# Low parts of the first network's hidden values: a subtraction on POOL or DVE replaced by an accumulating DMA, with the second layer one step later

## The chip, the cores and the metric

The kernel runs on one core of one Trainium2 chip. The metric is device microseconds of that core for one execution. Three executions of the kernel before took 1061.05, 1056.88 and 1058.72 us; their median is 1058.72 us.

## What is computed

The input `x` has two sequences of 3008 tokens with 256 features. The reference takes the real part of a two-dimensional Fourier transform and sends every token through two small networks:

```python
X = np.fft.fft(x, axis=1); X = np.fft.fft(X, axis=2); x = X.real     # 6016 tokens of 256
gate = 1 / (1 + np.exp(-(x @ w_gate))); val = x @ w_val              # 256 -> 1536, twice
x = (gate * val) @ w_out                                             # first network, 1536 -> 256
h = x @ w_in                                                         # 256 -> 2048
out = (h * np.cos(h)) @ w_out2                                       # second network, 2048 -> 256
```

The inputs are float32. TensorE is fed with `float32r` operands, which keep fewer bits, so each product is made of three matmuls: an operand is cut into a high part (the value rounded to `float32r`) and a low part (the value less its high part), and high times high, low times high and high times low are added up in PSUM.

## The kernel before, in words

**Fourier transform.** Up to about 85 us the core transforms the tokens in three stages (`stage_b` and `stage_c` are the last two); the last two blocks of `stage_c` are woven into the first two steps of the first network. The result stands in six tiles `eo` of 2 x 1004 columns, each of which holds 502 even and 502 odd combinations, that is, 1004 tokens.

**First network.** `step1(s)` runs once for each of 72 pairs (six token tiles, twelve blocks of 128 hidden features), s = 12 t + f, and for a few steps more that drain it. Each step issues, on TensorE: `ab(s, 0)`, 6 matmuls of 502 columns (lines L474 to L476) for the even half; `ab(s, 1)`, 6 for the odd half; and `out1(s - L1)`, 12 matmuls (L516 and L517 on the high part of the hidden values, L514 on the low part) of the second layer for the block that was made L1 = 3 steps earlier. These are 24 matmuls a step.

Between the two layers the block s passes over the other engines:

- `even(s)` on DVE (L492, two instructions of 502 columns) takes the even half out of PSUM into `sas`.
- `tokens(s)` on DVE (L500, two instructions of 2 x 502 columns) adds and subtracts the odd half; the result `gv[s]` holds gate and value of 1004 tokens. It frees the PSUM banks that `ab(s + 1, 1)` writes. There are three `gv` buffers.
- ACT takes the sigmoid of the gate (L652, 1004 columns), in place.
- `times(s)` on POOL (L504, two of 502 columns) multiplies value and gate. It is issued in step s + 1.
- `hi1(s)` on ACT (L591, two of 502 columns) rounds the product into the high part `gh[s][:, 0]`, issued in step s + 1, right behind the two halves of `times(s)`.
- `lo1(s, c, at)` (L529, two of 502 columns) subtracts the high part from the product into the low part `gh[s][:, 1]`, in step s + 2, on POOL, or on DVE where the planner's clock of POOL is late (`e = V if ... else G`).

**The planner.** The order of instructions is made by the Python program itself. It keeps an estimated clock per engine (`clk`, advanced by `spend`), and between the fixed work of a step it calls `fill` (through `ahead`) to put steps of the weight preparation on an engine as long as they end by a given time. The weights come as eight-byte words and are turned into float32 on the chip: 34 units (twelve `w1`, six `wo1`, sixteen `w2`, and one small one), each with one load by SP's queue, two ACT instructions (L117, L118), three on DVE (L121, L123, L125), one on POOL (L128), and a split into high and low part on ACT (L133) and POOL or DVE (L134). A unit needs a room: one of `stages`, four pieces of the tile `D1`, three of which stay open for the whole first network; earlier units also use the `eo` tiles. `need` issues at once what is left of a unit when a step must have it: `wo1` unit u by the step L1 + 2 u. The `w2` units are written to DRAM (`ws`) and loaded over the first network's weights in the last twelve steps (`w2_load`).

**Second network.** 192 steps of 12 matmuls each (`hid`, L474 to L476 again, and `out2`, L558), with the cosine on ACT and DVE and the split on ACT and POOL.

The lines that the change touches are `gvs`, `sas`, `ks` and `rs` (pieces of `D1`), the rooms at the stage "b05", `tokens`, `lo1`, `hi1` and `step1`. The lines of `step1` around the change:

```python
if 1 <= s <= N1S:
    ahead(G, gate_at)
    for c in (0, PC):
        times(p, c)                       # p = s - 1
        done[c] = spend(G, 1.3, gate_at) + .1
    if s > 1:
        hi1(p)
```

Of the kernel before, what the change touches and what calls it, by code (L numbers as in the profile page):

```python
# [14 lines left out]
ALU = mybir.AluOpType  # L15
# [7 lines left out]
PC = 502  # L23
NCH = 3
NPT = B * NCH
TW = 2 * PC
# [5 lines left out]
NRAW = NPRE = 6  # L32
NWARM = 5
CX0 = 4
L1, L2 = 3, 5

INV2PI = float(np.float32(1 / (2 * np.pi)))
C1 = 6.28125
# [5 lines left out]
UC = 512  # L44
# [5 lines left out]
def fft_moe_moe(ctx: ExitStack, tc: tile.TileContext, x, x0, head, w1, w1s, wo1, w2, t1, t3, out):  # L50
# [10 lines left out]
    V, A, G, PE = nc.vector, nc.scalar, nc.gpsimd, nc.tensor  # L61

    def f32(ap):
        return ap.bitcast(F32)
# [21 lines left out]
    flat1 = D1.rearrange("p c j -> p (c j)")  # L86
    stages = [flat1[:, i * 3 * UC:(i + 1) * 3 * UC] for i in range(4)]

    GV0 = 9 * UC
    gvs = [flat1[:, GV0 + i * 2 * TW:GV0 + (i + 1) * 2 * TW] for i in range(3)]  # L90
    sas = flat1[:, GV0 + 6 * TW:GV0 + 7 * TW].rearrange("p (g c) -> p g c", g=2)
    ks = [gvs[0][:, i * PC:(i + 1) * PC] for i in range(2)]
    rs = [gvs[0][:, 2 * PC:3 * PC], gvs[0][:, 3 * PC:4 * PC], gvs[1][:, 0:PC]]

    ctx.enter_context(tc.manual_schedule())

# [5 lines left out]
    clk = {V: 0.0, A: 0.0, G: 0.0, DQ: 0.0}  # L102
    VG = (V, G)

    def spend(e, us, after=0.0):
        clk[e] = max(clk[e], after) + us
        return clk[e]
# [58 lines left out]
    live = []  # L166
    free = []
# [27 lines left out]
    def fill(e, until):  # L195

        while True:
            for un in live:
                step = un[2][0]
                if step[0] is VG and e is G and max(un[3], clk[V]) + VADV < max(un[3], clk[G]):  # L200
                    continue
                if e in step[0] if step[0] is VG else e is step[0]:
                    if max(un[3], clk[e]) + cost(step, e) <= until:
                        step_of(un, e)
                        break
            else:
                if e is DQ and len(todo) > held[0] and clk[e] + 1.5 <= until:
                    for bf in free:
                        if bf[2] <= until and max(clk[e], bf[2]) + LIFE <= bf[1]:
                            start(bf)  # L210
                            break
                    else:
                        return
                    continue
                return
# [6 lines left out]
    def finish(un):  # L222
        while un in live:
            step_of(un)

    def need(key):

        at = 0.0
        while key in todo:
            if not free:  # L230
                finish(live[0])
            start(free[0])
        for un in list(live):
            if un[0] == key:
                finish(un)
                at = un[3]
        return at

    LIFE, ALWAYS = 16.0, 1e9
    VADV = 0.5  # L240
    ENDS = (44, 52, 54, 62, 70, 70)

# [8 lines left out]
    def split_eo(t):  # L251
        live.insert(0, [("es", t), None, split_steps(ess[t % 2], eo[t][:, :, 0:PC]), 0.0])
# [24 lines left out]
    with tc.tile_pool(name="xp", bufs=1) as xp:  # L277
# [29 lines left out]
        now = 3.5  # L307
# [139 lines left out]
    for st in "b00 b01 b02 b03 b04 c00 b05 b10 c01 b11 c02 b12 b13 b14 c10 b15".split():  # L447
        kind, b, i = st[0], int(st[1]), int(st[2])
        if st == "c10":
            nbank[:] = [3, 4]  # L450
        now = (stage_b if kind == "b" else stage_c)(b, i)
        if st == "b01":
            after.append(consts)
        if st == "b05":
            free += [[bf, ALWAYS, now] for bf in stages[:3]] + [[stages[3], now + 24, now]]
            split_eo(0)


# [1 line left out]
    MM = .2275  # L460

    LATE = {V: 1.2, G: 4.5, A: 2.0}
    LO_BY = 5.0
    ES_AT, PSTART, PACE, NW2 = 3, 7, 16 / 58, 16
    ys = {}

# [12 lines left out]
    N1S = NPT * NF1  # L479
    gv, gh = {}, {}  # L480

    def ab(s, k):

        t, f = divmod(s, NF1)
        e = ess[t % 2]
        for g in range(2):
            three(ps[:, 4 + 2 * k + g, 0:PC], W1[:, f, g, k, 0], W1[:, f, g, k, 1], e[:, 0, k], e[:, 1, k])
# [7 lines left out]

    def tokens(s):

        gv[s] = gvs[s % 3].rearrange("p (g c) -> p g c", g=2)
        for c, op in ((0, ALU.add), (PC, ALU.subtract)):
            V.tensor_tensor(out=gv[s][:, :, c:c + PC], in0=sas, in1=ps[:, 6:8, 0:PC], op=op)  # L500

    def times(p, c):
        m = slice(c, c + PC)
        G.tensor_tensor(out=gv[p][:, 1, m], in0=gv[p][:, 1, m], in1=gv[p][:, 0, m], op=ALU.mult)  # L504
# [17 lines left out]
            else:  # L522
                A.copy(dst, src)

    def lo1(p, c, at):

        e = V if max(clk[G], at) + 1.3 > now + LO_BY and clk[V] < now + 12 * MM else G
        m = slice(c, c + PC)
        e.tensor_tensor(out=gh[p][:, 1, m], in0=gv[p][:, 1, m], in1=f32(gh[p][:, 0, m]), op=ALU.subtract)  # L529
        lo_at[p] = spend(e, 1.2 if e is V else 1.3, at) + .1  # L530


    def w2_load(u):
# [53 lines left out]

    def hi1(p):
        gh[p] = wp.tile([128, 2, TW], F32R, tag="gh", name=f"gh{p}", bufs=3)
        for c in (0, PC):  # L590
            A.copy(gh[p][:, 0, c:c + PC], gv[p][:, 1, c:c + PC])  # L591
            hi_at[p, c] = spend(A, .61, done[c]) + .1

    hi_at, done = {}, {}

    def ahead(e, until):
        fill(e, until + LATE[e])

    even_at = tokens_at = 0.0
    lo_at = {}  # L600

    def step1(s, mid=None):

        nonlocal now, gate_at, even_at, tokens_at
        main = s < N1S
        while after:
            after.pop(0)()

        held[0] = max(NW2 - max(PACE * (s - PSTART), 0), 0)
        fill(DQ, now + 3)  # L610
        if main:
            now = max(now, even_at, need(("w1", s)))
            if s % NF1 == 0:
                now = max(now, need(("es", s // NF1)))
            ab(s, 0)
        else:
            need(("ys", 0))
            i = s - N1S
            hid(i)
            cos_a(i)  # L620
        p = s - 1
        if 1 <= s <= N1S:

            ahead(G, gate_at)
            for c in (0, PC):
                times(p, c)
                done[c] = spend(G, 1.3, gate_at) + .1
            if s > 1:
                hi1(p)
        if main:  # L630

            ahead(V, now + 3 * MM)
            even(s)
            spend(V, .73, now + 3 * MM + .1)
            even_at = spend(V, .73, now + 6 * MM + .1) + .1
            now = mid() if mid else now + 6 * MM
            now = max(now, tokens_at)
            ab(s, 1)
            now += 6 * MM
        if 2 <= s <= N1S + 1:  # L640
            for c in (0, PC):
                lo1(s - 2, c, max(now, hi_at.pop((s - 2, c))))
            gv.pop(s - 2)
        if main:
            ahead(V, now)
            for un in [un for un in live if un[1] and un[1][1] < ALWAYS]:
                finish(un)
            free[:] = [bf for bf in free if bf[1] == ALWAYS]
            tokens(s)
            tokens_at = spend(V, 2.4, now + .1) + .1  # L650
            ahead(A, tokens_at)
            A.activation(out=gv[s][:, 0], in_=gv[s][:, 0], func=AF.Sigmoid)  # L652
            gate_at = spend(A, 1.05, tokens_at) + .1
        else:
            for e in (A, V, G):
                ahead(e, now)
        if s >= L1:
            now = max(now, lo_at.pop(s - L1, 0)) + 12 * MM
        if s >= L1:
            need(("wo1", (s - L1) // 2))  # L660
            ends = (s - L1) % NF1 == NF1 - 1
            out1(s - L1, 0, False)
            if ends:
                out1(s - L1, 0, True)
            out1(s - L1, 1, False)
            if not ends:
                out1(s - L1, 0, True)
            out1(s - L1, 1, True)
            gh.pop(s - L1)
        if main and s % NF1 == ES_AT and s // NF1 + 1 < NPT:  # L670
            split_eo(s // NF1 + 1)
            if s < NF1:
                live.append(live.pop(0))
        if s == N1S - 10:
            ys[0] = ess[0]
            live.insert(0, [("ys", 0), None, split_steps(ess[0], eo[0][:, :, 0:PC]), 0.0])
        if not main:
            if i >= 1:
                cos_b(i - 1)
            if i >= 2:  # L680
                cos_c(i - 2)


        while loads and s - (N1S - NF1) >= (loads[0] if loads[0] < NF1 else L1 + 2 * (loads[0] - NF1) + 1):
            u = loads.pop(0)
            need(("w2", u))
            w2_load(u)


    gate_at = 0.0  # L690
    LIFE, VADV = 0.0, 100.0
    beside[0] = .5
    free[:] = [bf for bf in free if bf[1] == ALWAYS]
    step1(0)
    now = stage_c(1, 1, AHC)
# [3 lines left out]
    free[:] = [bf for bf in free if bf[1] == ALWAYS]  # L699
    wp = ctx.enter_context(tc.tile_pool(name="wp", bufs=1))  # L700
    ess.append(wp.tile([128, 2, 2, PC], F32R, name="es1"))
    hi1(0)
    for s in range(2, N1S + L1):
        step1(s)
    for s in range(L1, N2S + L2):
# [102 lines left out]
```

## Time and profile before

| quantity | value |
|---|---|
| median of three executions | 1058.72 us (1056.88 to 1061.05) |
| the profiled execution, its own time | 1058.09 us |
| its span, first to last instruction | 1056.2 us |
| TensorE busy | 1011.9 us, 96% |
| DVE, ACT, POOL busy | 850.2, 715.9, 754.6 us |
| mean granted TensorE clock | 0.983 of full speed |

The profile is of one execution. Spans count from its first instruction. A matmul's row is about 0.39 us long, but the matmuls overlap in the pipeline, so it is the distance of their starts that tells how fast they go. "PEclk" is the share of full clock that TensorE was granted. In a table by stages, "(x87)" counts the instructions that touch a stretch, and in a row of a timeline the square bracket tells how long the engine had been idle before and what it waited for.

### The profile page before, as it was taken

Reading aid. Unit: us, or ns where it says so; the run is one execution under the profiler, and the core shown is the slowest. Engines: PE = TensorE matmul, PEld = TensorE weight load, DVE = VectorE, ACT = ScalarE, POOL = GpSimd, SP = SyncE. Lnnn points to the kernel's source line nnn. Section 1 sums busy time; section 2 is a strip of 40 time slices with the busy share of each in tenths; the row PEclk is TensorE's granted clock in tenths of the full one; section 3 lists DMA queues with packets and bytes.
Section 4 is the critical chain, followed back from the end, with each engine's and each line's share of the span. In section 5 each row is a group of like instructions: output and inputs, shape, how many; then the busy total and the mean of one; then the engine's idle time right before and its main releaser. Section 6 shows DMA issues by size and latency. Waiting matters only on the chain.

```text
span 1056.2 us, 13156 instructions
## 1 busy us (share of the span) xinstructions
PE 1011.9 (96%) x4566; PEld 837.4 (79%) x4566; DVE 850.2 (80%) x1087; ACT 715.9 (68%) x1208; POOL 754.6 (71%) x538
## 2 busy tenths in 40 slices
PE   9888977998989999999999999999999999999998
PEld 9877856887777777878788888888888888888886
DVE  4699984899999999999977777777777777777775
ACT  4665442545445545464588988889888898888886
POOL 2687995898999898989946656557565565665753
PEclk9899997999999999999999999999999999999999
DMA  9621010012121112053400000000000000000000
GB/s 259 205 100 61 0 40 21 1 40 80 40 80 41 40 40 81 1 159 119 159 22 3 17 20 1 21 20 1 20 1 20 20 0 20 1 20 20 1 20 21
DMA packets 15587, 48.57 MB, mean 46 GB/s; under 512 B 2016, under 2 KB 5408, under 8 KB 15520
## 3 DMA queue, kind: packets, MB, share of 16 engines
q1 hardware_dynamic: 15296, 47.59, 13.8%
q8 instruction: 36, 0.59, 0.2%
q14 instruction: 31, 0.25, 0.1%
q10 hardware_dynamic: 224, 0.14, 0.0%
HBM read 33.16 MB, written 14.56 MB: 45 GB/s over the span
## 4 chain that ended last, share of the span: by engine, by line
PE 66%; DVE 14%; POOL 8%; issue 7%; ACT 3%; DMA 2%; DVEq 0%; SPq 0%; POOLq 0%; ACTq 0%
PE ps L558 25%; PE ps L474 11%; PE ps L475 10%; PE ps L476 10%; DVE D L500 6%; POOL D L504 5%; DVE D L492 3%; POOL gh L529 3%; PE ps L514 3%; PE ps L516 2%; PE ps L517 2%; DMA eo<-in_w_dram 2%; DVE gh L529 1%; ACT D L652 1%; PE ps L417 1%
## 5 line engine op out<-in xcount | busy, mean ns | idle before, releaser
L584 POOL TENSOR_TENSOR h<-D,h 128x502 fp32r<-128x502 f32 x191 | 288.5, 1510 | 209.5 <-ACT h L583 205.0
L558 PE MATMUL ps<-h,wr 128*128 128x502 f32 x1152 | 291.8, 389 | 0.0
L474 PE MATMUL ps<-es,wr 128*128 128x502 f32 x672 | 265.2, 395 | 13.8 <-DVE D L500 13.6
L475 PE MATMUL ps<-es,wr 128*128 128x502 f32 x672 | 262.5, 391 | 0.0
L476 PE MATMUL ps<-es,wr 128*128 128x502 f32 x672 | 261.3, 389 | 0.0
L558 PEld LDWEIGHTS ps<-h,wr 128*128 128x128 f32 x1152 | 217.4, 189 | 44.7
L504 POOL TENSOR_TENSOR D<-D 128x502 f32<-128x502 f32 x144 | 204.0, 1437 | 41.9 <-ACT D L652 41.9
L591 ACT CAST gh<-D 128x502 fp32r<-128x502 f32 x144 | 88.1, 614 | 199.1 <-POOL D L504 184.5
L569 DVE SCALAR_TENSOR_TENSOR D<-D,ps 128x502 f32<-128x502 int32 x192 | 130.2, 678 | 113.0 <-POOL h L584 109.6
L500 DVE TENSOR_TENSOR D<-D,ps 128x1004 f32<-128x1004 f32 x144 | 172.2, 1196 | 11.9 <-PE ps L476 6.4
L474 PEld LDWEIGHTS ps<-es,wr 128*128 128x128 f32 x672 | 127.0, 189 | 48.4 <-DVE D L500 22.0
L570 DVE SCALAR_TENSOR_TENSOR D<-D 128x502 f32<-128x502 int32 x192 | 145.6, 759 | 6.6
L476 PEld LDWEIGHTS ps<-es,wr 128*128 128x128 f32 x672 | 126.8, 189 | 26.6
L475 PEld LDWEIGHTS ps<-es,wr 128*128 128x128 f32 x672 | 127.1, 189 | 24.9
L568 ACT ACTIVATE D<-ps 128x502 int32<-128x502 f32 x192 | 113.0, 589 | 41.5 <-PE ps L476 39.5
L576 DVE TENSOR_TENSOR D<-D,ps 128x502 f32<-128x502 f32 x192 | 128.9, 672 | 12.8 <-ACT D L575 12.8
L574 ACT ACTIVATE D<-D 128x502 f32<-128x502 f32 x192 | 119.3, 621 | 15.3 <-DVE D L570 12.7
L516 PE MATMUL ps<-gh,wr 128*128 128x502 f32 x288 | 115.2, 400 | 13.8 <-ACT wr L133 10.7
L575 ACT ACTIVATE D<-D 128x502 f32<-128x502 f32 x192 | 120.2, 626 | 6.1
L529 POOL TENSOR_TENSOR gh<-D,gh 128x502 fp32r<-128x502 f32 x92 | 123.9, 1360 | 0.0
L492 DVE SCALAR_TENSOR_TENSOR D<-eo,w,ps 128x502 f32<-128x502 f32 x144 | 100.1, 732 | 23.7 <-PE ps L476 21.8
L583 ACT CAST h<-D 128x502 fp32r<-128x502 f32 x192 | 114.9, 598 | 0.2 <-DVE D L576 0.2
(87 smaller groups left out, 1123.3 us busy)
## 6 DMA issues: line engine op xcount, KB each, us to landing
D<-in_w_dram SPq DMA_DIRECT2D x17, 512.0 KB, 3.3
ws<-D SPq DMA_DIRECT2D x16, 512.0 KB, 2.6
wr<-ws SPq DMA_DIRECT2D x16, 512.0 KB, 3.7
out_dram<-D SPq DMA_DIRECT2D x24, 251.0 KB, 2.9
raw<-in_x_dram SPq DMA_DIRECT2D x15, 384.0 KB, 9.4
eo<-in_w_dram SPq DMA_DIRECT2D x11, 512.0 KB, 9.1
D<-in_wo_dram SPq DMA_DIRECT2D x6, 512.0 KB, 5.0
T<-in_t_dram SPq DMA_DIRECT2D x1, 320.0 KB, 10.6
```

The source lines that it names most:

```text
L474: PE.matmul(o, w_hi, m_hi, start=first, stop=False)
L475: PE.matmul(o, w_lo, m_hi, start=False, stop=False)
L476: PE.matmul(o, w_hi, m_lo, start=False, stop=last)
L492: V.scalar_tensor_tensor(out=sas[:, g], in0=eo[t][:, 0, PC:TW], scalar=w128[:, g * NF1 + f:g * NF1 + f + 1], in1=ps[:, 4 + g, 0:PC], op0=A ...
L500: V.tensor_tensor(out=gv[s][:, :, c:c + PC], in0=sas, in1=ps[:, 6:8, 0:PC], op=op)
L504: G.tensor_tensor(out=gv[p][:, 1, m], in0=gv[p][:, 1, m], in1=gv[p][:, 0, m], op=ALU.mult)
L516: PE.matmul(o, WO1[:, f, 0, m], h[:, 0, sl], start=(f == 0), stop=False)
L529: e.tensor_tensor(out=gh[p][:, 1, m], in0=gv[p][:, 1, m], in1=f32(gh[p][:, 0, m]), op=ALU.subtract)
L558: PE.matmul(o, WO2[:, f, i, d * 128:(d + 1) * 128], h[:, m], start=(f == 0 and i == m == 0), stop=(f == NF2 - 1 and m == 1))
L569: V.scalar_tensor_tensor(out=r, in0=k, scalar=-C1, in1=h, op0=ALU.mult, op1=ALU.add)
L570: V.scalar_tensor_tensor(out=r, in0=k, scalar=-C2, in1=r, op0=ALU.mult, op1=ALU.add)
L584: (V if s == N2S - 1 else G).tensor_tensor(out=h[:, 1], in0=r, in1=f32(h[:, 0]), op=ALU.subtract)
```

## The change

`lo1` no longer subtracts. ACT writes the high part and, in a second instruction, the negated product rounded in the same way, which is the negated high part, into the place of the low part; then an accumulating DMA, issued by POOL, adds the product itself onto it, which leaves the product less its high part. Each of the three is made once per step with 1004 columns (502 KB for the DMA). `hi1` and `lo1` of a block are issued two steps after the block's `ab` (`hi1` was issued one step after it). The second layer runs 4 steps behind the first rather than 3. The `gv` buffers are four and begin at the third of the four rooms of `D1`, so that two rooms stay open for weights; the other two are open up to step 1, and what stands in them is finished in step 2. The pieces that the second network's cosine uses move along.

```diff
--- before.py
+++ after.py
@@ -32,7 +32,7 @@
 NRAW = NPRE = 6
 NWARM = 5
 CX0 = 4
-L1, L2 = 3, 5
+L1, L2 = 4, 5
 
 INV2PI = float(np.float32(1 / (2 * np.pi)))
 C1 = 6.28125
@@ -86,11 +86,12 @@
     flat1 = D1.rearrange("p c j -> p (c j)")
     stages = [flat1[:, i * 3 * UC:(i + 1) * 3 * UC] for i in range(4)]
 
-    GV0 = 9 * UC
-    gvs = [flat1[:, GV0 + i * 2 * TW:GV0 + (i + 1) * 2 * TW] for i in range(3)]
-    sas = flat1[:, GV0 + 6 * TW:GV0 + 7 * TW].rearrange("p (g c) -> p g c", g=2)
-    ks = [gvs[0][:, i * PC:(i + 1) * PC] for i in range(2)]
-    rs = [gvs[0][:, 2 * PC:3 * PC], gvs[0][:, 3 * PC:4 * PC], gvs[1][:, 0:PC]]
+
+    GV0 = 6 * UC
+    gvs = [flat1[:, GV0 + i * 2 * TW:GV0 + (i + 1) * 2 * TW] for i in range(4)]
+    sas = flat1[:, GV0 + 8 * TW:GV0 + 9 * TW].rearrange("p (g c) -> p g c", g=2)
+    ks = [gvs[2][:, i * PC:(i + 1) * PC] for i in range(2)]
+    rs = [gvs[2][:, 2 * PC:3 * PC], gvs[2][:, 3 * PC:4 * PC], gvs[3][:, 0:PC]]
 
     ctx.enter_context(tc.manual_schedule())
 
@@ -237,6 +238,7 @@
         return at
 
     LIFE, ALWAYS = 16.0, 1e9
+    TWO = 1e8
     VADV = 0.5
     ENDS = (44, 52, 54, 62, 70, 70)
 
@@ -452,7 +454,7 @@
         if st == "b01":
             after.append(consts)
         if st == "b05":
-            free += [[bf, ALWAYS, now] for bf in stages[:3]] + [[stages[3], now + 24, now]]
+            free += [[bf, ALWAYS, now] for bf in stages[:2]] + [[bf, TWO, now] for bf in stages[2:]]
             split_eo(0)
 
 
@@ -460,7 +462,6 @@
     MM = .2275
 
     LATE = {V: 1.2, G: 4.5, A: 2.0}
-    LO_BY = 5.0
     ES_AT, PSTART, PACE, NW2 = 3, 7, 16 / 58, 16
     ys = {}
 
@@ -495,7 +496,7 @@
 
     def tokens(s):
 
-        gv[s] = gvs[s % 3].rearrange("p (g c) -> p g c", g=2)
+        gv[s] = gvs[(s + 2) % 4].rearrange("p (g c) -> p g c", g=2)
         for c, op in ((0, ALU.add), (PC, ALU.subtract)):
             V.tensor_tensor(out=gv[s][:, :, c:c + PC], in0=sas, in1=ps[:, 6:8, 0:PC], op=op)
 
@@ -522,12 +523,10 @@
             else:
                 A.copy(dst, src)
 
-    def lo1(p, c, at):
-
-        e = V if max(clk[G], at) + 1.3 > now + LO_BY and clk[V] < now + 12 * MM else G
-        m = slice(c, c + PC)
-        e.tensor_tensor(out=gh[p][:, 1, m], in0=gv[p][:, 1, m], in1=f32(gh[p][:, 0, m]), op=ALU.subtract)
-        lo_at[p] = spend(e, 1.2 if e is V else 1.3, at) + .1
+    def lo1(p, at):
+
+        G.dma_start(out=f32(gh[p][:, 1]), in_=gv[p][:, 1], accum_op=ALU.add)
+        lo_at[p] = spend(G, 1.2, at) + 4
 
 
     def w2_load(u):
@@ -587,11 +586,11 @@
 
     def hi1(p):
         gh[p] = wp.tile([128, 2, TW], F32R, tag="gh", name=f"gh{p}", bufs=3)
-        for c in (0, PC):
-            A.copy(gh[p][:, 0, c:c + PC], gv[p][:, 1, c:c + PC])
-            hi_at[p, c] = spend(A, .61, done[c]) + .1
-
-    hi_at, done = {}, {}
+        A.copy(gh[p][:, 0], gv[p][:, 1])
+        A.mul(gh[p][:, 1], gv[p][:, 1], -1.0)
+        return spend(A, 2.1, done.pop(p)) + .1
+
+    done = {}
 
     def ahead(e, until):
         fill(e, until + LATE[e])
@@ -618,15 +617,17 @@
             i = s - N1S
             hid(i)
             cos_a(i)
-        p = s - 1
+        if 3 <= s <= N1S + 1:
+            hi_at = hi1(s - 2)
         if 1 <= s <= N1S:
 
             ahead(G, gate_at)
             for c in (0, PC):
-                times(p, c)
-                done[c] = spend(G, 1.3, gate_at) + .1
-            if s > 1:
-                hi1(p)
+                times(s - 1, c)
+                done[s - 1] = spend(G, 1.3, gate_at) + .1
+        if 3 <= s <= N1S + 1:
+            lo1(s - 2, hi_at)
+            gv.pop(s - 2)
         if main:
 
             ahead(V, now + 3 * MM)
@@ -637,15 +638,11 @@
             now = max(now, tokens_at)
             ab(s, 1)
             now += 6 * MM
-        if 2 <= s <= N1S + 1:
-            for c in (0, PC):
-                lo1(s - 2, c, max(now, hi_at.pop((s - 2, c))))
-            gv.pop(s - 2)
         if main:
             ahead(V, now)
-            for un in [un for un in live if un[1] and un[1][1] < ALWAYS]:
+            for un in [un for un in live if un[1] and un[1][1] < (TWO if s < 2 else ALWAYS)]:
                 finish(un)
-            free[:] = [bf for bf in free if bf[1] == ALWAYS]
+            free[:] = [bf for bf in free if bf[1] == ALWAYS or bf[1] == TWO and s == 0]
             tokens(s)
             tokens_at = spend(V, 2.4, now + .1) + .1
             ahead(A, tokens_at)
@@ -699,7 +696,8 @@
     free[:] = [bf for bf in free if bf[1] == ALWAYS]
     wp = ctx.enter_context(tc.tile_pool(name="wp", bufs=1))
     ess.append(wp.tile([128, 2, 2, PC], F32R, name="es1"))
-    hi1(0)
+    lo1(0, hi1(0))
+    gv.pop(0)
     for s in range(2, N1S + L1):
         step1(s)
     for s in range(L1, N2S + L2):
```

## Rows read from the trace of the kernel before

**Rows 1.** The page's first part: busy us (share of the span) xinstructions.

```profile
PE 1011.9 (96%) x4566; PEld 837.4 (79%) x4566; DVE 850.2 (80%) x1087; ACT 715.9 (68%) x1208; POOL 754.6 (71%) x538
```

**Rows 2.** Table by stages: stretch and length; busy (instructions) PE, PEld, DVE, ACT, POOL; PEclk; DMA.

```profile
85.00:108.00 23.00, 20.10 (x87) 15.72 (x87) 20.55 (x25) 13.07 (x21) 16.89 (x14) 1.00 0.20 69
108.00:150.00 42.00, 40.96 (x180) 33.38 (x179) 39.84 (x43) 20.45 (x30) 39.09 (x29) 1.00 0.04 13
150.00:185.00 35.00, 23.98 (x79) 18.21 (x79) 17.16 (x19) 10.09 (x16) 21.08 (x17) 0.76 0.10 31
185.00:510.00 325.00, 312.04 (x1350) 252.19 (x1349) 307.69 (x315) 160.42 (x229) 297.05 (x217) 1.00 0.18 61
510.00:531.00 21.00, 18.59 (x75) 14.64 (x74) 18.32 (x16) 10.25 (x16) 18.27 (x13) 0.92 0.52 180
531.00:1052.00 521.00, 521.00 (x2296) 431.93 (x2294) 387.29 (x573) 451.76 (x799) 311.40 (x202) 1.00 0.03 12
```

**Rows 3.** Waits of TensorE, 84 to 531 us: total us, times, longest.

```profile
PE ps L474 <- DVE D L500: 13.6, 14, 1.6
PE ps L516 <- ACT wr L133: 10.7, 2, 5.6
PE ps L516 <- ACT eo L523: 3.1, 4, 1.3
PE ps L514 <- POOL gh L529: 2.4, 2, 1.7
```

**Rows 4.** Timeline of DVE ahead of one of those waits: start us, us, instruction.

```profile
238.87 1.38 DVE L492 SCALAR_TENSOR_TENSOR D<-eo,w,ps 128x502 f32<-128x502 f32 x2
240.17 3.40 DVE L529 TENSOR_TENSOR gh<-D,gh 128x502 fp32r<-128x502 f32 x2
243.49 2.42 DVE L500 TENSOR_TENSOR D<-D,ps 128x1004 f32<-128x1004 f32 x2
```

**Rows 5.** Timeline of TensorE: that wait, and one for `wo1` weights.

```profile
155.49 0.79 PE L516 MATMUL ps<-gh,wr 128*128 128x502 f32 x1 [5.05 <-ACT wr L133]
...
245.97 0.49 PE L474 MATMUL ps<-es,wr 128*128 128x502 f32 x1 [1.40 <-DVE D L500]
```

**Rows 6.** Groups by line, 185 to 510 us: count | busy us, mean ns | idle before.

```profile
L504 POOL TENSOR_TENSOR D<-D 128x502 f32<-128x502 f32 x112 | 158.4, 1435 | 26.4 <-ACT D L652 26.4
L500 DVE TENSOR_TENSOR D<-D,ps 128x1004 f32<-128x1004 f32 x113 | 135.1, 1196 | 8.1 <-PE ps L476 4.0 <-DVE D L125 0.2 <-ACT eo L523 0.2
L529 POOL TENSOR_TENSOR gh<-D,gh 128x502 fp32r<-128x502 f32 x67 | 90.8, 1367 | 0.0
...
L492 DVE SCALAR_TENSOR_TENSOR D<-eo,w,ps 128x502 f32<-128x502 f32 x112 | 77.8, 732 | 9.8 <-PE ps L476 8.2
L591 ACT CAST gh<-D 128x502 fp32r<-128x502 f32 x111 | 68.2, 614 | 152.3 <-POOL D L504 148.9 <-PE ps L514 3.3
L529 DVE TENSOR_TENSOR gh<-D,gh 128x502 fp32r<-128x502 f32 x43 | 62.7, 1471 | 0.0
...
L652 ACT ACTIVATE D<-D 128x1004 f32<-128x1004 f32 x56 | 58.3, 1040 | 14.9 <-DVE D L500 14.4
...
L128 POOL TENSOR_TENSOR D<-D 128x512 int32<-128x512 int32 x14 | 20.6, 1474 | 0.0
L125 DVE SCALAR_TENSOR_TENSOR D<-D 128x512 uint32<-128x512 uint32 x15 | 20.4, 1357 | 0.0
L134 POOL TENSOR_TENSOR D<-D 128x512 fp32r<-128x512 f32 x14 | 19.6, 1403 | 3.2 <-ACT D L133 2.6
L123 DVE TENSOR_SCALAR D<-D 128x512 uint32<-128x512 uint32 x16 | 15.0, 937 | 0.0
...
L121 DVE TENSOR_SCALAR D<-D 128x512 f32<-128x512 f32 x16 | 10.5, 659 | 0.0
```

**Rows 7.** The page's DMA issues: engine, count, KB each, us to landing.

```profile
ws<-D SPq DMA_DIRECT2D x16, 512.0 KB, 2.6
```

**Rows 8.** Timeline of SP's queue: one such issue.

```profile
395.30 0.33 SPq L161 DMA_DIRECT2D ws<-D  x1
```

## The prediction

> **What bounds the kernel now.** I read the page's busy line first: TensorE 96% of the span, DVE 80%, POOL 71% [rows 1]. TensorE is the bound on average, so the question is where its other time lies, and the table by stages answers it [rows 2]. In the second network (531 to 1052 us) 2296 matmuls stand in 521 us, 0.227 us each, and TensorE is busy throughout: nothing is to be had there. At that pace the stages before it lose: 85 to 108 us, 23 - 87 x 0.227 = 3.3 us; 108 to 150, 1.1; 150 to 185, 17.1; 185 to 510, 18.5; 510 to 531, 4.0. That is 44 us in all, and the most that this change can give back.
>
> The waits of TensorE name the causes [rows 3]. A wait's row starts at the modelled end of a 0.39 us matmul, so each costs some 0.16 us more than it shows, and a long one also costs clock: 150 to 185 us, with the two waits for ACT's L133, had a mean granted clock of 0.76 [rows 2].
>
> - 14 waits for `tokens` on DVE (L500). Two belong to the first steps, and in the timeline all twelve later ones have the same picture: one or two of the subtractions of `lo1` (L529) stand on DVE between `even` and `tokens`. One of them is shown: 3.40 us of L529, then 2.42 us of L500, then TensorE 1.40 us late [rows 4, 5].
> - Two waits of over 5 us for a `wo1` weight unit that was not yet decoded when its step came [rows 3, 5]. DVE and POOL had no room for it: from 185 to 510 us they are busy 307.7 and 297.1 of 325 us [rows 2]. That is a consequence of the same subtractions, which take 62.7 us of DVE and 90.8 us of POOL there [rows 6].
> - Four waits for `eo` (L523), issued on ACT behind a late sigmoid, and two at the end for the last low parts on POOL [rows 3].
>
> So the first network is a TensorE-bound loop that stumbles over DVE and POOL.
>
> **The change part by part.** I count per step; 185 to 510 us holds 112 / 2 = 56 steps [rows 6], 5.80 us each, against 24 x 0.227 = 5.45 us of matmuls.
>
> *DVE* loses L529. What stays is (135.1 + 77.8) / 56 = 3.80 us of `tokens` and `even`, and (20.4 + 15.0 + 10.5) / 56 = 0.82 us of weights [rows 6]: 4.62 of 5.45 us, where it now has 307.7 / 56 = 5.49.
>
> *ACT* exchanges two casts of 0.614 us for two instructions of 1004 columns, for which I take the sigmoid's 1.04 us: (160.4 - 68.2) / 56 + 2.08 = 3.73 us [rows 2, 6]. It stays covered. `hi1` moves a step back, so that ACT no longer waits for `times` (148.9 us of idle time ahead of L591 [rows 6]), and the sigmoid behind it in the queue comes earlier.
>
> *POOL* loses its share of L529 and gains one DMA issue per step. Without L529 it has (297.1 - 90.8) / 56 = 3.68 us. What the issue takes of POOL stands in no row, since POOL issues no DMA now. Bounds: 0.33 us, what SP's queue takes for a plain one [rows 8], and 2.73 us, the two instructions of 1.367 us that it replaces [rows 6]. I take 1.3, nearest to one of these two, since one instruction takes the place of two: POOL has 4.98 of 5.45 us. The issue waits on POOL for ACT's two instructions; queued behind it are weight work and the next `times`.
>
> [...] The rows show that the only float32 instructions of DVE from SBUF to SBUF with one input are L121 and L123, 16 each in the stage, (0.659 + 0.937) x 16 = 25.5 us [rows 6]; no row shows one beside a DMA issued by POOL. [...]
>
> *The transfer.* 502 KB each step, read from two places and written to one. A plain 512 KB store lands 2.6 us after its issue [rows 7]. Three streams (two reads, one write) against its two make one and a half times that, 3.9 us, my value; bounds are 2.6 and, for three passes of full length, 7.8. The room: call the start of step p + 2 zero. Sigmoid and `hi1` end at about 2.9, the two `times` of the next block at 3.8, the issue at 5.1, the landing at 9.0. TensorE wants the low part in step p + 4 at 2 x 5.45 + 2.73 + 1.8 = 15.4. Even 7.8 us leaves 2 us. The extra step of distance pays for the DMA; the waits that come with it, `tokens` for the buffer of four steps ago and L514 for the transfer, lie behind that room.
>
> *The weights.* Two rooms instead of three. A unit is due every 3.6 steps (16 in 58), so each may stay 7 steps, some 39 us; with 0.8 us of DVE and 0.5 us of POOL left free in each step the planner finds place sooner than now. The `wo1` units are due a step later, too. I expect both long waits to go, and cost the lost room at nothing; the cover is that free time, and without it a late unit costs what it costs now, some 8 us (half of 17.1).
>
> *The edges.* In the first steps there is no second layer, and DVE's 3.8 us against 2.7 us of matmuls set the pace. That stage keeps its 3.3 us, and a fourth step without `out1` adds 3.8 + 0.2 - 2.7 = 1.3, say 1.5 us. At the end the last DMAs must land behind ACT's work for the second network, while the last weights load: 2 us stay of 4 (0 to 6).
>
> **The sum.** Lost after the change: 3.3 + 1.5 at the start, 0 from 108 to 185 us, 4 of the 18.5 us from 185 to 510 (stray waits for `tokens` behind weight work and for `eo`), 2 at the end, 10.8 us. 44.0 - 10.8 = 33.2 us saved. The profiled execution took 1058.09 us, 0.6 below the median of three: 1058.1 - 33.2 = 1024.9, so 1025 us. Of the bounds, no loss at all but the start's gives 1019; some spread below that is in the pace itself.
>
> **Rivals.**
>
> *POOL becomes the bound (slower).* The place is POOL's queue in every step. With 2.73 us for an issue it has 3.68 + 2.73 = 6.41 us a step. The steps from 108 to 510 us take 402 / 67 = 6.00 us now (1609 matmuls, 24 each [rows 2]), so it decides from an issue of 2.3 us on: 67 x 0.41 = 27 us more, 1085 us. For it: POOL is 91% busy now and nothing shows the price. Against: it needs the whole of what is removed. 0.08. Near 2.2 us it gives back all that was won, and the time stays within 0.5%: 0.05.
>
> *The transfer is the bound.* If the accumulation kept the DMA engines for the full 7.8 us, each step would wait for its transfer: 67 x 1.8 = 121 us more, 1179 us. For it: three passes; against: the engines are 18% busy in this stage now [rows 2], and a transfer that merely lands late is covered. 0.05.
>
> *The waits are only moved.* DVE's place between `even` and `tokens` is filled by weight work in place of L529, or the two rooms delay the units so that the last ones are forced through in the end. If the 18.5 us of 185 to 510 us stay: 1025 + 14.5 + 4 for the end, about 1043 us. Against it: the weight work on DVE is the same as now, and the picture of the twelve waits. 0.14.
>
> *Held-up issues.* [...] 0.06. [...]
>
> **How the numbers follow.** My forecast (1015 to 1038) has 0.62, the held-up issues 0.06, the moved waits 0.14, no change 0.05, the two slower cases 0.13. Faster by over 0.5% (about what a measurement of this kernel can tell from no change) is 0.62 + 0.06 + 0.14 = 0.82. The range runs from 1015, a little below the bound without waits, to 1048, which takes in the moved waits.
>
> **What would show it.** Right: no L529 on DVE; the waits for L500 down from 14 to a few; no wait for L133; a granted clock of 1.00 from 108 to 510 us; steps of 5.5 us. DVE about 75 us less busy, ACT some 60 us more. The POOL price is right if its other instructions start some 1.3 us later around an issue. Wrong: POOL's instructions back to back with gaps of over 2 us for an issue, TensorE waiting at L514 for the DMA, or at L516 for a weight unit; a start later than 3 us against now would say that closing the two rooms in step 2 costs something.

## The result and the profile after

The changed kernel takes 1043.6 us (median of 4 runs, 1041.4 to 1046.3) against 1059.4 us before: ratio 0.985, interval 0.982 to 0.989. It is faster by 15.8 us; I had forecast 33.2 us. The time lies above my forecast of 1015 to 1038 us and inside the wider range to 1048, which was set to take in a rival. The profiled execution took 1041.4 us (span 1039.5).

The page's busy line, to be read beside [rows 1]:

```profile
PE 1005.1 (97%) x4566; PEld 838.0 (81%) x4566; DVE 780.4 (75%) x1033; ACT 765.0 (74%) x1207; POOL 668.0 (64%) x521
```

The load moved as planned: DVE 69.8 us less, POOL 86.6 less, ACT 49.1 more. Both engines that stood in TensorE's way have room now. The table by stages (columns as in [rows 2]) shows how little of that arrived:

```profile
85.00:108.00 23.00, 19.14 (x84) 14.66 (x82) 21.24 (x26) 12.82 (x18) 13.25 (x11) 1.00 0.24 68
108.00:150.00 42.00, 38.41 (x158) 31.73 (x159) 35.40 (x39) 25.25 (x30) 33.06 (x30) 0.92 0.53 112
150.00:185.00 35.00, 35.00 (x155) 29.05 (x154) 28.87 (x35) 24.14 (x29) 26.70 (x24) 1.00 0.60 134
185.00:510.00 325.00, 315.39 (x1355) 258.94 (x1354) 246.97 (x263) 200.90 (x232) 237.07 (x208) 0.98 0.69 161
510.00:531.00 21.00, 21.00 (x94) 17.32 (x93) 14.24 (x21) 17.08 (x30) 8.64 (x6) 1.00 0.21 43
```

The stages are fixed stretches of time. The length of a stretch less its matmuls at 0.227 us, as in the prediction, gives what TensorE loses in it:

| stage, us | before | forecast | after |
|---|---|---|---|
| 85 to 108 | 3.3 | 4.8 (with the fourth step) | 3.9 |
| 108 to 150 | 1.1 | 0 | 6.1 |
| 150 to 185 | 17.1 | 0 | -0.2 |
| 185 to 510 | 18.5 | 4 | 17.4 |
| 510 to 531 | 4.0 | 2 | -0.3 |
| sum | 44.0 | 10.8 | 26.9 |

So the gain is in the main what the two long waits for `wo1` weights (150 to 185 us) and the end of the network cost before, less 5.0 us more lost from 108 to 150. In the 325 us of the long stage TensorE issues 1355 matmuls instead of 1350: hardly any gain, with DVE 60.7 us less busy there. TensorE's waits from 84 to 531 us:

```profile
PE ps L475 <- DVE D L501: 10.9, 6, 4.2
PE ps L475 <- DVE D L493: 5.3, 4, 2.9
PE ps L515 <- DMA gh<-D: 0.9, 1, 0.9
```

Against [rows 3] the waits for L133, for `eo` and for POOL's `gh` are gone, and the waits for `tokens` (now L501) went from 14 to 6, but they are longer, and four waits for `even` (L493) are new. What makes DVE late with so much room? One of the four places, first DVE (timeline: start us, us, instruction):

```profile
257.70 0.88 DVE L122 TENSOR_SCALAR D<-D 128x512 f32<-128x512 f32 x1
258.61 5.37 DVE L124 TENSOR_SCALAR D<-D 128x512 uint32<-128x512 uint32 x1
263.90 1.37 DVE L493 SCALAR_TENSOR_TENSOR D<-eo,w,ps 128x502 f32<-128x502 f32 x2
```

POOL in the same stretch:

```profile
257.62 1.19 POOL L528 DMA_DIRECT2D gh<-D  x1
258.22 1.70 POOL L135 TENSOR_TENSOR es<-eo,es 128x502 fp32r<-128x502 f32 x1
259.47 1.69 POOL L135 TENSOR_TENSOR D<-D 128x512 fp32r<-128x512 f32 x1
260.73 2.87 POOL L505 TENSOR_TENSOR D<-D 128x502 f32<-128x502 f32 x2
263.17 1.27 POOL L528 DMA_DIRECT2D gh<-D  x1
```

and TensorE behind it:

```profile
264.68 0.50 PE L475 MATMUL ps<-es,wr 128*128 128x502 f32 x1 [1.34 <-DVE D L493]
...
267.96 0.79 PE L475 MATMUL ps<-es,wr 128*128 128x502 f32 x1 [1.66 <-DVE D L501]
268.55 0.62 PE L476 MATMUL ps<-es,wr 128*128 128x502 f32 x1
268.96 0.62 PE L477 MATMUL ps<-es,wr 128*128 128x502 f32 x1
```

A weight instruction that elsewhere takes 0.43 us takes 5.37, and it ends 0.38 us after the last of four POOL computations that stand end to end (260.73 + 2.87 = 263.60). `even` and `tokens` stand behind it on DVE, so TensorE waits twice, and after the second wait its matmuls start 0.41 us apart instead of 0.23: the granted clock is 0.50 from 268 to 273 us, and 1.00 again from 276 to 280. Four rows are like that: L122 at 105.77 (3.42 us), L124 at 195.86 (4.58), L124 at 258.61 and L122 at 324.87 (5.42). By the starts of TensorE's matmuls, 2.9, 6.2 and 6.3 us are lost behind the last three, 15.4 of the 17.4 us of the long stage, and the loss of 108 to 150 us follows the first.

The other terms, in the groups of 185 to 510 us, beside [rows 6]:

```profile
L505 POOL TENSOR_TENSOR D<-D 128x502 f32<-128x502 f32 x112 | 145.3, 1358 | 75.2 <-ACT D L649 75.2
L590 ACT ACTIVATE gh<-D 128x1004 fp32r<-128x1004 f32 x57 | 59.3, 1040 | 0.0
L589 ACT CAST gh<-D 128x1004 fp32r<-128x1004 f32 x57 | 58.1, 1019 | 1.0 <-PE ps L515 1.0
L528 POOL DMA_DIRECT2D gh<-D x57 | 54.1, 949 | 12.2 <-issue 6.7 <-ACT D L573 3.1 <-POOL D L505 1.4
L124 DVE TENSOR_SCALAR D<-D 128x512 uint32<-128x512 uint32 x13 | 15.8, 1217 | 0.4
L122 DVE TENSOR_SCALAR D<-D 128x512 f32<-128x512 f32 x13 | 11.6, 892 | 0.7 <-ACT D L118 0.7
L126 DVE SCALAR_TENSOR_TENSOR D<-D 128x512 uint32<-128x512 uint32 x13 | 9.3, 714 | 0.0
```

An issue takes 0.95 us of POOL (I took 1.3), ACT's two instructions 1.02 and 1.04 us (I took 1.04). The transfer, in the page's list (beside [rows 7]) and in the view of L528:

```profile
gh<-D POOLq DMA_DIRECT2D x72, 502.0 KB, 4.7
```

```profile
DMA to landing us min/median/max: 4.4/4.7/10.1
```

4.7 us against the 3.9 that I took. From the start of an issue to the first low matmul there are 11.8 us in the median and 7.2 at the least, and TensorE waited for the transfer at one step (0.9 us, the last wait above).

### The profile page after: what moved, and what is told of

It reads as the page before. It is cut to its first block, busy times and chain, and to the rows that moved or that the text cites. A ratio compares the mean times of both kernels' runs of the same rounds, so it can differ in the third digit from the quotient of the medians.

```text
span 1039.5 us, 13150 instructions
## 1 busy us (share of the span) xinstructions
PE 1005.1 (97%) x4566; PEld 838.0 (81%) x4566; DVE 780.4 (75%) x1033; ACT 765.0 (74%) x1207; POOL 668.0 (64%) x521
## 4 chain that ended last, share of the span: by engine, by line
PE 73%; DVE 4%; ACT 2%; DMA 1%; issue 1%; POOL 0%; DVEq 0%; ACTq 0%
PE ps L557 25%; PE ps L475 12%; PE ps L476 12%; PE ps L477 12%; PE ps L515 4%; PE ps L517 4%; PE ps L518 4%; DVE D L501 3%; DMA gh<-D 1%; ACT gh L589 1%; DVE D L124 1%; DVE D L122 1%; ACT gh L590 1%; DVE D L493 0%; ACT eo L524 0%
## 5 line engine op out<-in xcount | busy, mean ns | idle before, releaser
L583 POOL TENSOR_TENSOR h<-D,h 128x502 fp32r<-128x502 f32 x191 | 284.3, 1489 | 215.8 <-ACT h L582 204.1
L475 PE MATMUL ps<-es,wr 128*128 128x502 f32 x672 | 265.6, 395 | 16.1 <-DVE D L501 10.9
L505 POOL TENSOR_TENSOR D<-D 128x502 f32<-128x502 f32 x144 | 186.3, 1352 | 93.0 <-ACT D L649 93.0
L501 DVE TENSOR_TENSOR D<-D,ps 128x1004 f32<-128x1004 f32 x144 | 172.9, 1201 | 51.6 <-PE ps L477 30.0
L649 ACT ACTIVATE D<-D 128x1004 f32<-128x1004 f32 x72 | 75.1, 1044 | 149.8 <-DVE D L501 149.8
L493 DVE SCALAR_TENSOR_TENSOR D<-eo,w,ps 128x502 f32<-128x502 f32 x144 | 101.8, 736 | 32.7 <-PE ps L477 32.3
L517 PE MATMUL ps<-gh,wr 128*128 128x502 f32 x288 | 114.3, 397 | 0.0
L518 PE MATMUL ps<-gh,wr 128*128 128x502 f32 x288 | 113.4, 394 | 0.0
```

Source lines behind the costliest of these rows:

```text
L475: PE.matmul(o, w_hi, m_hi, start=first, stop=False)
L517: PE.matmul(o, WO1[:, f, 0, m], h[:, 0, sl], start=(f == 0), stop=False)
L518: PE.matmul(o, WO1[:, f, 1, m], h[:, 0, sl], start=False, stop=False)
L583: (V if s == N2S - 1 else G).tensor_tensor(out=h[:, 1], in0=r, in1=f32(h[:, 0]), op=ALU.subtract)
```

## The experiments

The first theory: while POOL issues the accumulating DMA, or because of the way its instructions then stand (in the rows above each starts before the one ahead of it ends), DVE's `tensor_scalar` (L122 and L124, the clamp and the shift of the weight preparation) is kept from starting. The first four kernels test it.

**The same DMA as a plain copy, issued by SP.** The low part is then the whole product.

```diff
-        G.dma_start(out=f32(gh[p][:, 1]), in_=gv[p][:, 1], accum_op=ALU.add)
+        nc.sync.dma_start(out=f32(gh[p][:, 1]), in_=gv[p][:, 1])
```

> The transfer of each step is a plain copy of the product, issued by SP's queue; POOL issues no DMA (the low part is then the whole product). Theory: the lost time comes from POOL's issue, behind which POOL's rows overlap and DVE's TENSOR_SCALAR (L122, L124) gets no turn; without an issue on POOL no such row is longer than 1.6 us, the waits for L493 and L501 after 108 us are nearly gone, and the time is 1041.4 - 22 = about 1019 us (1014 to 1026). Rival, the transfer's traffic slows DVE: the same bytes still move each step, rows of 3 to 5 us stay and the time is 1036 to 1046. Rival, the place of the weight work in DVE's queue: 1036 to 1046 too, with short rows.

Measured: 1021.0 us, ratio 0.964 (0.961 to 0.967). No `tensor_scalar` takes over 1.41 us, and TensorE's waits from 84 to 531 us are down to

```profile
PE ps L475 <- DVE D L501: 4.2, 3, 2.0
PE ps L475 <- DVE D L493: 0.2, 1, 0.2
```

all in the first steps. The rows stay in the same place of DVE's queue and are short now, so neither that place nor the bytes moved each step made them long. With POOL free of the issue the rest of the change gives 1021 us, against the 1025 that I had forecast.

**A plain copy issued by POOL.** Same line, `G.dma_start` without `accum_op`; the low part is the whole product here too.

> The transfer is issued by POOL as in the changed kernel, but copies without adding (the low part is then the whole product). Theory: as in the changed kernel, some TENSOR_SCALAR rows of 3 to 5.5 us, POOL's rows overlapping by some 0.3 us behind an issue, 1036 to 1046 us. If the adding is what matters: no such rows, about 1019 us.

Measured: 1037.4 us, ratio 0.980 (0.977 to 0.983). The issue takes 0.58 us instead of 0.87 (medians), and the long rows are there again. DVE and then POOL:

```profile
321.03 5.45 DVE L122 TENSOR_SCALAR D<-D 128x512 f32<-128x512 f32 x1 [0.42 <-ACT D L118]
```

```profile
319.96 0.58 POOL L528 DMA_DIRECT2D gh<-D  x1 [1.62 <-issue]
320.56 1.29 POOL L135 TENSOR_TENSOR es<-eo,es 128x502 fp32r<-128x502 f32 x1
321.79 1.30 POOL L135 TENSOR_TENSOR D<-D 128x512 fp32r<-128x512 f32 x1
323.05 2.50 POOL L505 TENSOR_TENSOR D<-D 128x502 f32<-128x502 f32 x2
325.50 0.58 POOL L528 DMA_DIRECT2D gh<-D  x1
```

POOL's rows do not run into one another here (320.56 + 1.29 = 321.85, the next starts at 321.79), so the overlap is not the cause. The accumulation itself costs some 6 us (1043.6 - 1037.4).

**The subtraction on POOL, no DMA at all.** One instruction of 1004 columns; ACT's negated copy is dropped, and the planner's prices stay, so that the order of the rest does too.

```diff
-        G.dma_start(out=f32(gh[p][:, 1]), in_=gv[p][:, 1], accum_op=ALU.add)
+        G.tensor_tensor(out=gh[p][:, 1], in0=gv[p][:, 1], in1=f32(gh[p][:, 0]), op=ALU.subtract)
...
-        A.mul(gh[p][:, 1], gv[p][:, 1], -1.0)
```

> The changed kernel without the DMA and without ACT's negated copy: POOL subtracts, one instruction of 1004 columns; one step more of distance, four gate-value buffers, two rooms and the order stay. Theory: no TENSOR_SCALAR row over 1.6 us, since POOL issues no DMA; but POOL has 4.23 - 0.94 + 2.2 = 5.5 us a step against 5.45 and becomes the bound here and there, 1025 to 1045 us. Rival, any long run of POOL instructions keeps DVE out: rows of 3 us and more stay and are more frequent, over 1045 us.

Measured: 1095.1 us, ratio 1.034 (1.030 to 1.038), slower than both kernels. L122 now waits up to 10.4 us with no DMA on POOL:

```profile
PE ps L475 <- DVE D L493: 37.3, 10, 9.2
```

```profile
308.41 10.42 DVE L122 TENSOR_SCALAR D<-D 128x512 f32<-128x512 f32 x1
318.87 0.43 DVE L124 TENSOR_SCALAR D<-D 128x512 uint32<-128x512 uint32 x1
```

POOL's last row ahead of its end:

```profile
316.20 2.35 POOL L528 TENSOR_TENSOR gh<-D,gh 128x1004 fp32r<-128x1004 f32 x1
```

POOL has run without a gap from 305.43 to 318.55 us, and L122 ends 0.28 us later. The theory of the issue falls: the long rows need no DMA on POOL, and the rival stated beforehand (any long run of POOL's instructions keeps DVE out) is what came. What remains is POOL's computation: L122 waited here until it paused.

**The weights' two operations in a form with one operand in PSUM.** Two spare columns of a PSUM bank hold the second constants; the values are the same, and the new form holds from the first step of the first network on. The clamp, in part (`...` stands for lines left out):

```diff
+    cmax = ps[:, 7, 510:511]
...
+        if one_port[0]:
+            V.scalar_tensor_tensor(out=t, in0=t, scalar=FMIN, in1=cmax.to_broadcast([128, n]),
+                                   op0=ALU.max, op1=ALU.min)
...
-            (V, .34, lambda: V.tensor_scalar(out=t, in0=t, scalar1=FMIN, scalar2=FMAX,
-                                             op0=ALU.max, op1=ALU.min)),
...
+            (V, .34, lambda: clamp(t, n)),
...
+    one_port[0] = True
     step1(0)
```

and L124's shift in the same way.

> The changed kernel, but from the first network's first step on the two TENSOR_SCALAR of a weight unit are SCALAR_TENSOR_TENSOR with the second constant read from a spare PSUM column; the order of all instructions stays. Theory: these rows take 0.6 to 0.8 us and none is over 1.6, POOL is untouched, the waits of TensorE for L493 and L501 after 108 us nearly go, 1018 to 1026 us. Rival, the place of the weight work in DVE's queue or the two rooms: the waits stay, 1036 to 1046 us.

Measured: 1025.6 us, ratio 0.969 (0.966 to 0.972). The waits of TensorE, and the long stage of the table:

```profile
PE ps L492 <- DVE D L518: 6.5, 4, 2.0
PE ps L532 <- DMA gh<-D: 2.2, 2, 1.3
PE ps L492 <- DVE D L510: 0.2, 1, 0.2
```

```profile
185.00:510.00 325.00, 321.07 (x1406) 264.52 (x1405) 247.76 (x274) 209.33 (x247) 238.44 (x210) 1.00 0.69 162
```

1406 matmuls in the stage instead of 1355. By stages it loses 2.1 + 1.8 - 0.2 + 5.8 - 0.3 = 9.2 us, where the forecast had 10.8; the single terms differ by up to 2.7 us and partly cancel. The order of all instructions is that of the changed kernel, so the place of the weight work in DVE's queue, the rival here, is not what cost it. This version beats both kernels. The direction that the prediction had weighed, DVE holding up POOL's issues, cost nothing that shows: with the old form and with the new an issue takes 0.87 us and its transfer lands in 4.7 and 4.9 us (medians).

**The same form with the subtraction on POOL.** This was to separate two causes of the 1095 us.

> The kernel with POOL's subtraction of 1004 columns (1095.1 us, ten waits of TensorE for L493 on DVE, 37.3 us in all), with nothing altered but the form of the two DVE operations of the weight units: the second constant is read from a PSUM column, so that they run as scalar_tensor_tensor. Theory (a two-operation tensor_scalar from SBUF to SBUF is kept waiting by a long run of POOL's instructions, and everything behind it on DVE with it): the rows of 6.5 to 10.4 us are gone, the two new rows stay near 0.7 us each, the waits for L493 are under 5 us in all, and the time falls by at least 40 us, to 1055 us or less. Rival (POOL, with 2 x 1.28 + 2.40 us a step and its weight work, is simply too full for a step of 5.46 us, and DVE is late only as a consequence): TensorE still waits, now for POOL's L528, and the time stays above 1085 us.

Measured: 1078.3 us, ratio 1.019 (1.015 to 1.022). Neither expectation holds: 17 us came back, not 40, and TensorE's waits for `even` still are 28.6 us in all, and none is for POOL's subtraction. The groups of weight instructions on DVE, 95 to 531 us, say why. First POOL's subtraction with the old form, then with the new one:

```profile
L122 DVE TENSOR_SCALAR D<-D 128x512 f32<-128x512 f32 x19 | 79.9, 4206 | 6.6 <-ACT D L118 6.6
L126 DVE SCALAR_TENSOR_TENSOR D<-D 128x512 uint32<-128x512 uint32 x19 | 23.6, 1244 | 0.0
L124 DVE TENSOR_SCALAR D<-D 128x512 uint32<-128x512 uint32 x19 | 21.7, 1143 | 0.6
```

```profile
L143 DVE SCALAR_TENSOR_TENSOR D<-D 128x512 uint32<-128x512 uint32 x19 | 85.0, 4474 | 0.0
L123 DVE SCALAR_TENSOR_TENSOR D<-D,ps 128x512 uint32<-128x512 uint32 x19 | 13.1, 687 | 1.6 <-PE ps L494 1.0
L116 DVE SCALAR_TENSOR_TENSOR D<-D,ps 128x512 f32<-128x512 f32 x19 | 13.0, 682 | 4.3 <-ACT D L137 4.0 <-PE ps L494 0.3
```

The two altered ones (D and ps as inputs) take 0.69 and 0.68 us in the mean, the same as with the DMA (0.69 and 0.68 in the changed kernel with the new form). The third, which reads two operands from SBUF, waited little before (1.24 us in the mean) and is now the one that waits, up to 10.2 us. So my theory was too narrow. Not only `tensor_scalar` is kept out (with one input it needs 0.42 us from SBUF to SBUF where the new form needs 0.68 for the same columns), but also a DVE instruction with two inputs in SBUF. One with an SBUF and a PSUM operand was not held up in any of these kernels: the rows of `even` keep within 4% from 85 to 531 us, those of `tokens` within 2% (0.72 to 0.74 and 1.18 to 1.20 us before and after the change). In the changed kernel with the new form L143 was held for long only once (4.53 us).

**The kernel before with the new form**, as a control.

> The kernel before, with the same alteration of form alone. In its trace no tensor_scalar takes over 1.6 us, since each gets in at the first end of a POOL instruction. Theory (the form matters only where an operation is passed over several times): the time stays within 0.7% of the kernel before, 1052 to 1067 us. Rival (the form is a gain by itself: the kernel before loses to it too, 0.8 us mean against 0.42 us when nothing is in the way, and POOL's next row is 0.2 us longer): 1045 us or less, so that a part of what the changed kernel gains from the form has nothing to do with the change.

Measured: 1050.6 us, ratio 0.992 (0.990 to 0.994): between the two expectations, so neither holds. In the kernel before hardly any DVE instruction is held past the first end of a POOL instruction (1 of 75, table below). But the waits of up to 1.1 us for that end (L123 takes 0.42 us at the least and 1.55 at the most) seem to count, too, where DVE is busy for all of a step: TensorE's waits for `tokens` fall from 13.6 us to 7.9. The form is worth 8 us before the change and 18 after it (1043.6 - 1025.6). If it is worth the same 8 in both, the other 10 are what the change brought on; no run shows that split.

**The slack alone:** four buffers, a lag of 4 steps and two rooms, but `lo1` as before, in halves on DVE or POOL.

> The changed kernel with its fourth buffer, its lag of 4 steps and its two rooms for weights, but the low parts by the subtraction of before, 502 columns at a time, on DVE or POOL by the rule of before (no negated copy on ScalarE, no DMA). It tells the slack from the move. Theory (the subtraction on DVE, 0.87 us a step, ahead of even and tokens is what held TensorE): DVE is back at 5.5 us a step, the waits for L501 come back, and the time is 1045 us or more. Rival (the fourth step and buffer are what gain, since the subtraction no longer has a due time close to its issue): 1035 us or less, no slower than the changed kernel.

Measured: 1049.6 us, ratio 0.991 (0.989 to 0.993). The time and the waits are those of the theory; DVE has 293.85 us in the long stage, 5.2 a step and not 5.5. TensorE waits 13 times for `tokens`, nearly as often as before:

```profile
PE ps L476 <- DVE D L502: 17.7, 13, 3.6
PE ps L518 <- ACT wr L134: 5.7, 1, 5.7
```

One of the two weight waits went with the slack; the other is gone only in the changed kernel, where the subtraction has left DVE and POOL, too. The slack alone is worth 9.2 us (1058.8 - 1049.6), more than half of the whole gain of 15.8: while the held rows stay, moving the subtraction adds only some 6 us.

**A lag of 3 steps** (`L1, L2 = 3, 5`), all else of the change kept.

> The changed kernel with the second layer 3 steps behind in place of 4, nothing else altered. In the changed kernel the first low matmul comes 10.2 us (median) after the issue of its accumulating DMA, the least 6.4, and the DMA lands in 4.7 us (4.4 to 10.1). One step less takes 5.46 us of that. Theory (the fourth step is needed to cover the landing): the median margin is gone (10.2 - 5.5 - 4.7 = 0.0 us), TensorE waits for the DMA at many steps, over 10 us in all, and the time is 1050 us or more. Rival (the low part is used late enough in the step that the lag does not matter, and the held-up DVE rows set the time as before): waits for the DMA under 4 us, time 1038 to 1047 us.

Measured: 1054.6 us, ratio 0.996 (0.994 to 0.998). The theory holds: without the fourth step the transfer is uncovered at eight steps. The 10.2 us in the expectation should be 11.8, counted from the start of an issue, so that 1.6 us of the median margin are left rather than none; it is the late transfers that TensorE waits for.

```profile
PE ps L515 <- DMA gh<-D: 16.7, 8, 5.5
```

**POOL's subtraction in halves**, to see what makes DVE lose its turn. I counted the DVE instructions of the two kinds above that found POOL at work, 85 to 531 us ("held up"), and those of them that were still waiting after the first end of a POOL instruction ("passed over"). The counts move by several with the point at which a wait is taken to begin. The last column, the longest row of the two kinds, needs no such choice and shows the same contrast.

| kernel | held up | of these passed over | longest row, us |
|---|---|---|---|
| before / with the new form / slack alone | 75 / 58 / 76 | 1 / 1 / 1 | 1.84 / 1.87 / 1.85 |
| DMA by SP | 7 | 0 | 1.86 |
| after / plain copy by POOL / lag 3 / new form | 19 / 9 / 11 / 8 | 5 / 5 / 3 / 1 | 5.42 / 5.45 / 7.13 / 4.53 |
| subtraction on POOL, 1004 columns: old form / new | 38 / 23 | 8 / 8 | 10.42 / 10.23 |
| subtraction on POOL, 2 x 502 columns | 41 | 9 | 10.91 |

> The kernel with POOL's subtraction once more (1095.1 us with one instruction of 1004 columns, 2.40 us), now as two instructions of 502 columns, nothing else altered. It asks what makes DVE lose its turn. In the kernel before and in the one with the slack alone, where POOL runs 502 and 512 columns at a time and DVE takes part of the subtraction, a DVE instruction that found POOL at work got in at the first end of a POOL instruction 74 times of 75 and 75 of 76; with the long subtraction it was passed over 8 times of 38. Theory A (the long instruction is what does it): passed over at most once, waits of TensorE for L493 under 10 us in all, and the time falls to 1070 us or less, POOL's 5.1 us of subtraction and multiplication a step alone being left. Theory B (it goes by how full POOL is, not by the length of its instructions): passed over 6 times or more, rows over 6 us, and the time stays within 1.5% of 1095 us.

Measured: 1107.7 us, ratio 1.043 (1.037 to 1.049). The length of the instruction is not what decides: with the halves, too, DVE was passed over 9 times, and waited up to 10.9 us. The numbers of theory B came, but not its reason, since POOL's mean load does not decide it either. Here are the slack alone and then these halves, 108 to 510 us (POOL fifth, then clock and DMA):

```profile
108.00:510.00 402.00, 380.71 (x1626) 309.28 (x1626) 358.25 (x375) 181.39 (x212) 382.12 (x282) 0.98 0.16 57
```

```profile
108.00:510.00 402.00, 343.23 (x1373) 273.90 (x1372) 341.74 (x285) 156.31 (x185) 348.97 (x278) 0.91 0.12 41
```

With the slack alone POOL is busier, 95% against 87%, in instructions of the same width, and DVE was passed over once in 76. In most cases a DVE instruction that was passed over then waited until POOL paused or issued a DMA: the rows of 5.37, 5.45 and 10.42 us above end 0.38, 0.93 and 0.28 us after the last computation of such a run. What decides whether it gets in at the first end stays open; the moment of its arrival, the spacing of POOL's rows and the waits of either instruction did not tell the two kinds apart.

## Why the prediction was wrong, and where it was right

*Right.* What bounds the kernel: a TensorE loop that stumbles over DVE and POOL. There is no L529 on DVE and no wait for L133, and both long `wo1` waits are gone (17.3 us, forecast 17.1); the slack alone removes one of them. The prices held: by the 57 issues of the long stage DVE has 246.97 / 57 = 4.33 us a step (forecast 4.62), ACT 3.52 (3.73), POOL 4.16 (4.98, of which the issue 0.95 for 1.3). The transfer needs the fourth step and is covered by it. Two rooms for weights cost no wait: no unit was late. The rivals of a full POOL and of a bounding transfer did not come.

*Wrong: the term "4 of the 18.5 us from 185 to 510 (stray waits for `tokens` behind weight work)" and the 0 for 108 to 150.* They measured 17.4 and 6.1, 19.5 us more than forecast; the start and the edges gave 3 back. The step that failed is the overlap behind these terms: "0.82 us of weights [rows 6]" let DVE's weight work run beside POOL at a mean length, so that nothing long could stand ahead of `even` and `tokens`. The runs show single weight rows held for 3.42 to 5.42 us behind POOL, `even` and `tokens` queued behind them, and part of the loss at the lower clock: 0.92, 1.00 and 0.98 in the three stages from 108 to 510 us where the prediction's sign was 1.00.

The trace of before held the warning. I took the means of L121, L123 and L125 as prices, and they contain waits (least, median and longest, in ns):

```profile
L121 DVE TENSOR_SCALAR D<-D x23: 414/420/1494, 71.0 to 500.8; 128x512 f32<-128x512 f32 x23
L125 DVE SCALAR_TENSOR_TENSOR D<-D x23: 684/1634/1839, 72.0 to 512.0; 128x512 uint32<-128x512 uint32 x23
```

A mean of 0.66 or 1.36 us on such an instruction says that something stands in its way, and the mean sets no bound to a single wait. The same goes for the subtraction itself: L529 on DVE has 0.67 us as its least row and 1.47 as its mean [rows 6], so that much of the 62.7 us that the change takes from DVE was waiting, too.

The rival "the waits are only moved" named the right place, weight work ahead of `tokens`, and I gave it 0.14 on the ground that "the weight work on DVE is the same as now". Its work was; its waiting was not. Its cause did not come: in the same place and order the weight work cost next to nothing with the DMA on SP (1021.0 us) or in the new form (1025.6). That its price of about 1043 us is the measured time is in part luck: the 4 us that it added for the end did not come (-0.3 us there), and 6.1 us from 108 to 150, which it did not have, made up for them.

I weighed the hold-up in one direction only, DVE against POOL's issues (and called L123 a float32 instruction; its rows say uint32). The 0.06 that I gave it was an estimate of mine, and no run shows that direction: with the old form and with the new an issue took 0.87 us, and its transfer landed in 4.7 and 4.9 us. The runs show POOL holding up DVE. Held were `tensor_scalar` from SBUF to SBUF (up to 10.9 us, 0.42 at the least) and the instruction with two SBUF inputs (L143, up to 10.2); not held were those with one SBUF and one PSUM operand (the new form at 0.68 us in the mean, `even` within 4%). Why the line runs there no row shows. With the halves the L122 row of 10.70 us at 309.92 us was passed over at eight ends of POOL instructions and got in after the ninth.

## What to carry to other kernels

When an instruction's longest row is several times its least, read the difference as a wait, look for the engine whose instruction ends just before it does, and ask what the change does to that engine. Work that stands in order ahead of a critical instruction should have a form whose rows stay short beside the other engines: an operand in PSUM at 0.68 us instead of 0.42 made the whole kernel 18 us faster. And taking work off a late engine gains only as much as that work made it late: in the long stage DVE lost 60.7 us of busy time, and TensorE gained five matmuls.

## What was not expected of the hardware

- DVE instructions of 0.42 us took up to 10.9 us beside an unbroken run of POOL instructions, and up to 7.1 us in kernels with DMA issues on POOL; with one operand from PSUM they took 0.68 us in the mean.
- An accumulating DMA of 502 KB took 0.87 us of POOL to issue and landed in 4.7 us (medians); the plain copy took 0.58 us to issue and landed in 2.9.
- While DVE was held behind four POOL instructions at 258.61 us, POOL's own rows were 1.6 to 1.7 us long instead of 1.3, each starting 0.4 to 0.6 us before the one ahead of it ended; with the plain copy they stayed at 1.3, and DVE was held all the same.
